# The output product of a soft mixture of experts: 16 small float32 tiles in place of two passes of a rounded pair

## The chip, the core and the metric

The kernel runs on one core of a Trainium2 chip. A core has a matrix engine (TensorE, PE in the profile; its weight loads are shown apart as PEld), a vector engine (VectorE, DVE), a scalar engine (ScalarE, ACT), GpSimd (POOL) and a queue that issues transfers (SyncE, SP). Each engine works through its own instructions in order and waits on semaphores for the others. TensorE writes to PSUM, 128 partitions of eight banks of 512 float32 values; everything else lives in SBUF, the on-chip memory. The metric is the device time in microseconds of one execution; a profiled execution also gives a span, from the first to the last instruction.

## The reference

The input `x` has shape (8, 2496, 256). The real part of its two-dimensional Fourier transform is the token matrix of a soft mixture of experts with eight experts of four slots:

```python
X = np.fft.fft(np.fft.fft(x, axis=1), axis=2).real   # reshaped to N = 19968 rows of 256
logits = X @ phi                                      # N x 32
d = softmax of logits over the rows;  slot_input = d.T @ X        # 32 x 256
for e in range(8):                                    # four slots each
    slot_out[e] = relu(slot_input[e] @ w1[e]) @ w2[e]
c = softmax of logits over the 32 slots
return c @ slot_out                                   # N x 256
```

Both softmaxes add 1e-9 to the denominator. Only the last line is computed differently by the change: a product of N x 32 weights with a 32 x 256 matrix, which writes 20.45 MB.

## The kernel before

The eight sequences are handled as four pairs `p` = 0 to 3. The kernel never forms the transformed tokens. It works on folded input, gets the logits of a pair (`lt[p]`) through small transforms, collects the slot inputs, runs the experts, and then weights the expert outputs for every token.

The code is cut into parts, `a`, `t`, `b`, `c`, `e`, `d`, `u` for the transforms and sums of a pair, `m`, `l`, `v` for the experts, and four that matter here. The string `ORDER` lists them in the order in which they are written, and a scheduler with a time model then sets the order on each engine.

- `part_r` takes the finished slot outputs `so` from PSUM (L508, L509), repeats them with one product (`sorep`, L510), and builds the right-hand matrices `rh`. They are in float32r, a format that TensorE takes in one pass; since it is rounded, `rh[0]` holds the value and `rh[1]` what the rounding lost (L515), each with two copies of the 32 x 256 matrix on a block diagonal.
- `part_s(p)` is the softmax over the slots: eleven TensorE transposes of the logits into three PSUM banks (`cT`, L529), three ScalarE copies into `c` (L534), and then for each of two halves a maximum (VectorE, L543), a subtract (POOL, L544), an exponential (ScalarE, L545), a sum, an addition and a reciprocal (VectorE, L546 to L548), and a product (POOL, L549).
- `part_q(p, i)` splits half `i` of `c` into a float32r value (ScalarE, L555) and its residual (VectorE, L556), side by side in `hl`.
- `part_o(p, b)` is one chunk of output, five for each pair. Four TensorE transposes turn a block of `hl` into weights (`lT`, L569), ScalarE copies them to SBUF (`lTs`, L570), and four times two products with `rh` (L576) fill one bank each, `po`, 128 x 512. VectorE and ScalarE copy the banks in turn to a buffer `o` (L580), and SP sends it (L587, L585), 1 MiB for a whole chunk.

The buffers `o` come from a ring of six; they are reused when their transfer has landed. PSUM is split into pools that live through the whole kernel: `ps` (two banks), `ps3` (three), `p1` (two) and `u` (one). The products `po` use `ps` and `ps3`, the transposes `cT` and `lT` use `p1`.

In `ORDER` the end reads `... q00 s10 v00 v10 r00 o00 q01 o01 q10 o02 o03 o04 o10 s20 q11 o11 ...`: the softmaxes of pairs 0 and 1 come ahead of the experts' end, those of pairs 2 and 3 between the chunks.

Of the kernel before, what the change touches and what calls it, by code (L numbers as in the profile page):

```python
# [116 lines left out]
def _build(nc, tc, xh, phih, w1h, w2h, cins, where, out, out0):  # L117
# [4 lines left out]
    with ctx:  # L122
        cp = ctx.enter_context(tc.tile_pool(name="cp", bufs=1))
        sb = ctx.enter_context(tc.tile_pool(name="sb", bufs=1))
        pp = ctx.enter_context(tc.tile_pool(name="pp", bufs=P2, space=PSUM))
# [373 lines left out]

        def part_r():  # L500
            so = sos_[0]
            for j in range(2):
# [5 lines left out]
            sc.copy(sos[:, :128], so[:, :128])  # L508
            v.tensor_copy(sos[:, 128:], so[:, 128:D])  # L509
# [2 lines left out]
            sc.copy(rh[0][half[0], 0, :], ps[half[0], :D])
# [8 lines left out]

        def part_s(p):
            L = lt[p]
            cq[p] = sb.tile([128, 40, NSLOT], F32, name=f"c{p}", tag=CT[p], bufs=bufs_(CT[p]))
# [13 lines left out]
            e1 = nc.gpsimd if GP & 1 else v  # L538
            e2 = nc.gpsimd if GP & 2 else v
            for i in range(2):  # L540
# [3 lines left out]
                e1.tensor_tensor(c, c, m[:, 0].unsqueeze(2).to_broadcast([128, 20, NSLOT]), op=ALU.subtract)  # L544
# [4 lines left out]
                e2.tensor_tensor(c, c, m[:, 1].unsqueeze(2).to_broadcast([128, 20, NSLOT]), op=ALU.mult)  # L549

        def part_q(p, i):
            c = cq[p][:, 20 * i : 20 * i + 20]
            e3 = nc.gpsimd if GP & 4 else v
# [2 lines left out]
            e3.tensor_tensor(t[:, :, 1], c, t[:, :, 0].bitcast(F32), op=ALU.subtract)  # L556
# [4 lines left out]

        def part_o(p, b):
            ps = bank1(f"lT{p}_{b}", F32R)
            lT = et([128, 4, 128], f"lTs{p}_{b}", F32R)
            with tc.issue_after(anchor["v1"]) if LA and p == 0 else nullcontext():
              for i in range(4):
                k0 = 8 * b + 2 * i
                src = hl[p, k0 // 20][:, k0 % 20 : k0 % 20 + 2].rearrange("p k h s -> p (k h s)")
                pe.transpose(ps[:, i * 128 : i * 128 + 128], src, identr)  # L569
            sc.copy(lT, ps.rearrange("p (i n) -> p i n", i=4))  # L570
# [87 lines left out]
```

## Time and profile before

| | us |
|---|---|
| three runs of the kernel | 199.41, 200.8, 201.35 |
| the profiled execution | 201.22 |
| its span | 199.4 |
| PE busy (share of the span) | 174.7 (88%) |
| DVE busy | 131.8 (66%) |
| ACT busy | 132.4 (66%) |
| POOL busy | 24.6 (12%) |
| experts' last product ends, about | 139.5 |
| first output transfer is issued | 143.90 |
| last output transfer is issued | 190.89 |

The profile's rows give an engine, a line of the kernel, the operation, output and input tiles and a count, and then times: in the groups, busy us and mean ns of one, and the engine's idle time ahead of them with what ended it; in the timeline and the chain, start and length in us. A busy TensorE is not TensorE at its peak, since matmuls overlap and their ends are modelled.

### The profile page before, as it was taken

What the parts mean: (1) busy time and instruction counts of PE and PEld (TensorE: products, weight loads), DVE (VectorE), ACT (ScalarE), POOL (GpSimd) and SP (SyncE); (2) the same over time, 40 slices, a digit from 0 to 9 for tenths busy, and PEclk for the clock granted to TensorE, in tenths of its full rate; (3) what the DMA queues carried; (4) which work ended last, traced back from release to release, by engine and by line L of the source; (5) the groups of instructions that cost most, each with busy time, mean ns of one, the idle gap of its engine ahead of it and who ended that gap; (6) DMA issues with size and microseconds to landing.
All of it is one profiled execution on the core that took longest, in us unless ns stands there. A gap on an engine that the chain in (4) does not pass through costs nothing.

```text
span 199.4 us, 4290 instructions
## 1 busy us (share of the span) xinstructions
PE 174.7 (88%) x1690; PEld 125.6 (63%) x1690; DVE 131.8 (66%) x238; ACT 132.4 (66%) x277; POOL 24.6 (12%) x27
## 2 busy tenths in 40 slices
PE   0499889969999999989999989999999999989900
PEld 0375575549666877556865859346788877768700
DVE  0599856989993991742357624796677888976700
ACT  2135775579876795687856963763867988896610
POOL 0000000000000000000000100767101357320000
PEclk9999999997999999999999999999999999999995
DMA  5999999998880499600393687991099999799996
GB/s 183 409 427 410 422 420 420 419 391 291 301 363 21 112 358 424 263 0 0 111 283 138 205 326 234 364 404 58 2 378 355 419 409 389 306 421 363 430 426 214
DMA packets 10707, 59.17 MB, mean 297 GB/s; under 512 B 1344, under 2 KB 1728, under 8 KB 5696
## 3 DMA queue, kind: packets, MB, share of 16 engines
q1 hardware_dynamic: 10688, 58.91, 76.0%
q8 instruction: 13, 0.21, 0.4%
q14 instruction: 6, 0.05, 0.1%
HBM read 38.46 MB, written 20.45 MB: 295 GB/s over the span
## 4 chain that ended last, share of the span: by engine, by line
PE 75%; ACT 10%; DMA 2%; DVE 2%; issue 2%; POOL 2%; SPq 0%; ACTq 0%; DVEq 0%; POOLq 0%
PE po L576 17%; PE pt L231 9%; PE z L238 7%; PE a L275 6%; PE e L331 6%; PE u L373 5%; PE d L348 4%; PE h L472 4%; PE so L492 3%; PE lp L293 3%; PE lm L294 3%; PE cT L529 2%; DMA x<-xh 2%; ACT zt L262 2%; PE lT L569 2%
## 5 line engine op out<-in xcount | busy, mean ns | idle before, releaser
L576 PE MATMUL po<-rh,lTs 128*128 128x512 f32 x160 | 42.4, 405 | 1.5 <-ACT lTs L570 0.7
L231 PE MATMUL pt<-cs,eo 128*128 128x128 f32 x160 | 26.9, 300 | 8.9 <-DVE eo L226 7.9
L576 PEld LDWEIGHTS po<-rh,lTs 128*128 128x128 f32 x160 | 28.1, 188 | 8.5 <-ACT o L580 1.8
L232 ACT COPY et<-pt 128x512 f32<-128x512 f32 x40 | 23.1, 592 | 13.8 <-PE pt L231 13.2
L580 DVE COPY o<-po 128x512 f32<-128x512 f32 (+1 forms) x40 | 26.9, 686 | 7.9 <-PE po L576 7.0
L231 PEld LDWEIGHTS pt<-cs,eo 128*128 128x128 f32 x160 | 19.9, 153 | 15.9 <-DVE eo L226 7.9
L580 ACT COPY o<-po 128x512 f32<-128x512 f32 x40 | 23.2, 595 | 7.3 <-PE po L576 7.1
L224 DVE TENSOR_TENSOR x<-x 128x1024 f32<-128x1024 f32 x16 | 19.5, 1217 | 3.0 <-DMA x<-xh 3.0
L238 PE MATMUL z<-et,wphi 128*32 128x256 f32 (+1 forms) x288 | 19.0, 371 | 1.9 <-ACT et L232 1.8
L544 POOL TENSOR_TENSOR c<-c,cm 128x640 f32<-128x640 f32 x8 | 11.8, 1489 | 28.0 <-DVE cm L543 27.0
L316 ACT ACTIVATE d<-lt,nm 120x128 f32<-120x128 f32 x44 | 13.6, 390 | 1.9 <-DVE nm L313 1.8
L226 DVE TENSOR_TENSOR eo<-x 128x512 f32<-128x512 f32 x20 | 13.6, 682 | 0.6 <-PE u L373 0.3
L238 PEld LDWEIGHTS z<-et,wphi 128*32 128x32 f32 x288 | 7.8, 113 | 9.4 <-ACT et L232 4.2
L227 DVE TENSOR_TENSOR eo<-x 128x512 f32<-128x512 f32 x20 | 13.6, 680 | 0.0
L331 PE MATMUL e<-cs,dpm 120*64 120x120 f32 x176 | 13.5, 273 | 0.0
L331 PEld LDWEIGHTS e<-cs,dpm 120*64 120x64 f32 x176 | 10.7, 136 | 3.5 <-issue 2.4
L356 ACT COPY ds<-d 64x320 f32<-64x320 f32 x24 | 10.0, 421 | 4.2 <-PE d L348 3.5
L275 PE MATMUL a<-cs,zt 128*120 128x128 f32 x88 | 12.2, 292 | 0.4 <-ACT zt L266 0.3
L275 PEld LDWEIGHTS a<-cs,zt 128*120 128x120 f32 x88 | 11.1, 196 | 1.9 <-ACT zt L266 1.3
L549 POOL TENSOR_TENSOR c<-c,cm 128x640 f32<-128x640 f32 x8 | 11.0, 1391 | 10.0 <-DVE cm L548 5.5
L570 ACT CAST lTs<-lT 128x512 fp32r<-128x512 f32 x20 | 11.5, 599 | 0.9 <-PE lT L569 0.9
L373 PE MATMUL u<-eo,ds 128*32 128x129 f32 x320 | 11.6, 275 | 0.0
(99 smaller groups left out, 251.4 us busy)
## 6 DMA issues: line engine op xcount, KB each, us to landing
x<-xh SPq DMA_DIRECT2D x16, 1024.0 KB, 11.3
out<-o SPq DMA_DIRECT2D x15, 1024.0 KB, 5.6
w<-w1h SPq DMA_DIRECT2D x6, 1024.0 KB, 8.6
w<-w2h SPq DMA_DIRECT2D x12, 512.0 KB, 6.0
x<-xh SPq DMA_DIRECT2D x4, 896.0 KB, 10.3
out<-o SPq DMA_DIRECT2D x4, 768.0 KB, 6.0
w<-w1h SPq DMA_DIRECT2D x4, 512.0 KB, 5.2
w<-w2h SPq DMA_DIRECT2D x2, 1024.0 KB, 8.0
```

The lines of the kernel that those rows point to most:

```text
L224: v.tensor_tensor(x[:, 0:4], x[:, 0:4], x[:, 4:8], op=ALU.add)
L226: v.tensor_tensor(e[:, :, 0:128], x[:, 0:4, 0:128], x[:, 0:4, 128:256], op=ALU.add)
L227: v.tensor_tensor(e[:, :, 128:256], x[:, 0:4, 0:128], x[:, 0:4, 128:256], op=ALU.subtract)
L231: pe.transpose(b[:, g * 128 : g * 128 + 128], e[:, g, k * 128 : k * 128 + 128], ident)
L232: sc.copy(tr[k][:, :, :, qi, :], b.rearrange("p (g h a) -> p g h a", g=4, h=2))
L238: pe.matmul(z[32 * g : 32 * g + 32, o : o + n], wphi[:, w, :], tr[k][:, g].rearrange("p h q a -> p (h q a)"), start=i != 1, stop=i != 0, t ...
L275: pe.matmul(ps[:120, i * 128 : i * 128 + 128], zt[p][:, GS * g : GS * g + GS].rearrange("p s h c -> p (s h c)"), C("wa"), start=True, stop ...
L316: sc.activation(d[:, g], L[:, g], AF.Exp, bias=nm[:, g : g + 1], scale=1.0)
L331: pe.matmul(ps[64 * k : 64 * k + 64, 120 * i : 120 * i + 120], dpm[p, hf][:, k, 3 * j + i, :], C(name), start=True, stop=True, tile_positi ...
L373: last = pe.matmul(ub[32 * g : 32 * g + 32, 0:129], dsb[p][:, k, c, :], e[:, 0:129] if k == 0 else e[:, 127:256], start=cc == 0, stop=cc == 9,
L576: pe.matmul(po, lT[:, i, :], rh[j].rearrange("p k d -> p (k d)"), start=j == 0, stop=j == 1,)
L580: (v.tensor_copy if n_ev[0] % 2 else sc.copy)(ot[:np_, 2 * i : 2 * i + 2, :].rearrange("p k d -> p (k d)"), po[:np_])
```

## The change

The output product is done in plain float32, with 32 x 32 tiles of the array. `part_q` is one VectorE transpose of a half of `c`, which turns 32 x 32 blocks and leaves them where they are, so that the slots of quarter `q` of the partitions come to lie on partitions 32q to 32q + 31 (`tl`). `part_o` then has 32 products for each chunk: row tile `q` takes 32 weights' rows on the partitions of quarter `q` and the copy of the slot outputs that lies there (`rep`), column tile `j` writes 32 partitions, and row tile `q` writes bank `q`. A chunk fills a slot of four banks; ScalarE copies banks 0 and 1, VectorE banks 2 and 3, 1024 values wide each. The two slots take all eight banks, so the pools from before are closed in `part_r`, and the logits' transposes of pairs 2 and 3 (`cT2`, `cT3`) use such a slot too. The splitting into value and residual, the identity in float32r, the `lT` transposes and their copies go. The order of rows in the output buffer differs, and the host puts them in place.

```diff
+        def four(name):
+            return p4[0].tile([128, 4, 512], F32, name=name, tag="p4")
...
         def part_r():
...
-            sc.copy(rh[0][half[0], 0, :], ps[half[0], :D])
-            (v.tensor_copy if RH else sc.copy)(rh[0][half[1], 1, :], ps[half[1], :D])
-            for k, r in enumerate(half):
-                v.tensor_tensor(rh[1][r, k, :], ps[r, :D], rh[0][r, k, :].bitcast(F32), op=ALU.subtract)
+            sc.copy(rep[:, :128], ps[:, :128])
+            v.tensor_copy(rep[:, 128:], ps[:, 128:D])
+            rep_.append(rep)
+            banks.close()
+            p4.append(ctx.enter_context(tc.tile_pool(name="p4", bufs=2, space=PSUM)))
...
         def part_s(p):
+            whole = four(f"cT{p}") if p4 else None
             for b in range(3):
-                ps = bank1(f"cT{p}_{b}")
+                ps = whole[:, b] if p4 else bank1(f"cT{p}_{b}")
...
         def part_q(p, i):
-            sc.copy(t[:, :, 0], c)
-            e3.tensor_tensor(t[:, :, 1], c, t[:, :, 0].bitcast(F32), op=ALU.subtract)
+            if i == 0:
+                tl[p] = se([128, 2 * NKC, NSLOT], f"tl{p}")
+            half = slice(20 * i, 20 * i + 20)
+            v.transpose(
+                tl[p][:, half].rearrange("p k n -> p (k n)"), cq[p][:, half].rearrange("p k n -> p (k n)")
+            )
...
         def part_o(p, b):
-            for i in range(4):
-                po = (bank, bank3)[i % 2](f"po{p}_{b}_{i}")
-                for j in range(2):
-                    pe.matmul(
-                        po, lT[:, i, :], rh[j].rearrange("p k d -> p (k d)"), start=j == 0, stop=j == 1,
+            po = four(f"po{p}_{b}")
+            for gi in range(2):
+                for j in range(4):
+                    for q in range(4):
+                        r = slice(32 * q, 32 * q + 32)
+                        pe.matmul(
+                            po[32 * j : 32 * j + 32, q, 256 * gi : 256 * gi + 256],
+                            tl[p][r, 8 * b + 4 * gi + j, :], rep[r, :],
+                            start=True, stop=True, tile_position=(32 * q, 32 * j),
+                        )
...
+            for i, ev in ((0, sc.copy), (1, v.tensor_copy)):
+                src = po[:, 2 * i : 2 * i + 2]
+                if b < 4 or i == 0:
+                    ev(ot[:, 4 * i : 4 * i + 4].rearrange("p k d -> p (k d)"), src.rearrange("p q n -> p (q n)"))
```

Three places in the engines' orders, with what each instruction waits for (a semaphore bears the name of the engine that raises it; DMAHW are transfers). First VectorE where the experts end and the output begins, before; `c1` are the weights of pair 1, `so` the slot outputs:

```order
L546 TENSOR_REDUCE cm1_1_1598<-c1_1572 128x20 [waits Activation_49]
L547 TENSOR_SCALAR cm1_1_1598<-cm1_1_1598 128x20 [waits DVE_49]
L548 RECIPROCAL cm1_1_1598<-cm1_1_1598 128x20 [waits DVE_49]
L556 TENSOR_TENSOR hl1_0_1740<-c1_1572,hl1_0_1740 128x20x32 [waits Activation_49]
L509 COPY sos_1676<-so_1606 128x128 [waits Activation_49]
L515 TENSOR_TENSOR rh1_1673<-sorep_1677,rh0_1671 64x256 [waits PE_49,Activation_49]
```

And there after the change:

```order
L543 TENSOR_REDUCE cm1_1_1596<-c1_1570 128x20 [waits Activation_49]
L553 STREAM_TRANSPOSE tl1_1759<-c1_1570 128x640 [waits Pool_49]
L544 TENSOR_SCALAR cm1_1_1596<-cm1_1_1596 128x20 [waits DVE_49]
L545 RECIPROCAL cm1_1_1596<-cm1_1_1596 128x20 [waits DVE_49]
L553 STREAM_TRANSPOSE tl1_1759<-c1_1570 128x640 [waits Pool_49]
L509 COPY sos_1669<-so_1604 128x128 [waits Activation_49]
L512 COPY rep_1670<-sorep_1671 128x128 [waits Activation_49]
```

Both transposes of pair 1, which wait for POOL, now stand ahead of the copy of `so`; before, the second half's subtract stood behind it. Second, the softmax of pair 2, on VectorE before; `po1_1_1` is a bank of the second chunk of pair 1:

```order
L543 TENSOR_REDUCE cm2_0_1862<-c2_1844 128x20 [waits Activation_49]
L543 TENSOR_REDUCE cm2_1_1870<-c2_1844 128x20 [waits DVE_49]
L580 COPY o1_0_1826<-po1_0_1_1831 128x512 [waits DMAHW3_49,DMAHW0_49,PE_49]
L580 COPY o1_0_1826<-po1_0_3_1839 128x512 [waits PE_49]
L580 COPY o1_1_1888<-po1_1_1_1893 128x512 [waits DMAHW3_49,DMAHW2_49,DMAHW4_49,DVE_49,PE_49]
L580 COPY o1_1_1888<-po1_1_3_1901 128x512 [waits PE_49]
L546 TENSOR_REDUCE cm2_0_1862<-c2_1844 128x20 [waits Activation_49]
L580 COPY o1_2_1916<-po1_2_1_1921 128x512 [waits DMAHW5_49,DVE_49,PE_49]
```

And there after, up to the copy of the third chunk of pair 1:

```order
L540 TENSOR_REDUCE cm2_0_1926<-c2_1910 128x20 [waits Activation_49]
L540 TENSOR_REDUCE cm2_1_1934<-c2_1910 128x20
L543 TENSOR_REDUCE cm2_0_1926<-c2_1910 128x20 [waits Activation_49]
L544 TENSOR_SCALAR cm2_0_1926<-cm2_0_1926 128x20 [waits DVE_49]
L545 RECIPROCAL cm2_0_1926<-cm2_0_1926 128x20 [waits DVE_49]
L543 TENSOR_REDUCE cm2_1_1934<-c2_1910 128x20 [waits Activation_49]
L575 COPY o1_1_1976<-po1_1_1943 128x1024 [waits DMAHW3_49,DMAHW2_49,Activation_49]
L544 TENSOR_SCALAR cm2_1_1934<-cm2_1_1934 128x20 [waits DVE_49]
L553 STREAM_TRANSPOSE tl2_1980<-c2_1910 128x640 [waits Pool_49]
L545 RECIPROCAL cm2_1_1934<-cm2_1_1934 128x20 [waits DVE_49]
L553 STREAM_TRANSPOSE tl2_1980<-c2_1910 128x640 [waits Pool_49]
L575 COPY o1_2_2015<-po1_2_1982 128x1024 [waits DMAHW4_49,Activation_49]
```

Before, copies of chunks stand between the steps of the softmax, and each waits for PE. After, all steps up to the second sum stand ahead of the next chunk's copy, and that copy waits for ScalarE's copy of the same chunk. ScalarE at the same place, before:

```order
L580 COPY o1_0_1826<-po1_0_0_1827 128x512 [waits DMAHW3_49,DMAHW0_49,PE_49]
L545 ACTIVATE c2_1844<-c2_1844 128x640 [waits Pool_49]
L580 COPY o1_0_1826<-po1_0_2_1835 128x512 [waits PE_49]
L570 COPY lTs1_3_1935<-lT1_3_1934 128x512 [waits PE_49]
L545 ACTIVATE c2_1844<-c2_1844 128x640 [waits Pool_49]
L580 COPY o1_1_1888<-po1_1_0_1889 128x512 [waits DMAHW3_49,DMAHW2_49,DMAHW4_49,DVE_49,PE_49]
```

And after:

```order
L575 COPY o1_0_1906<-po1_0_1873 128x1024 [waits DMAHW3_49,DMAHW0_49,PE_49]
L533 COPY c2_1910<-cT2_1911 128x40x12 [waits PE_49] x2
L533 COPY c2_1910<-cT2_1911 128x40x8 [waits PE_49]
L542 ACTIVATE c2_1910<-c2_1910 128x640 [waits Pool_49] x2
L575 COPY o1_1_1976<-po1_1_1943 128x1024 [waits DMAHW2_49,DMAHW3_49,DVE_49,PE_49]
```

Here too a chunk's copy now stands behind both exponentials. Third, TensorE at the logits' transposes of pair 2, before:

```order
L576 MATMUL po0_3_2_1784<-rh0_1671,lTs0_3_1769 128x512 [waits Activation_49]
L576 MATMUL po0_3_2_1784<-rh1_1673,lTs0_3_1769 128x512
L529 MATMUL cT2_1_1851<-cs0_70,lt2_943 128x120 [waits PE_49,Activation_49]
L529 MATMUL cT2_1_1851<-cs0_70,lt2_943 128x120 x3
L529 MATMUL cT2_2_1857<-cs0_70,lt2_943 128x120 [waits Activation_49]
L529 MATMUL cT2_2_1857<-cs0_70,lt2_943 128x120 x2
```

And after:

```order
L528 MATMUL cT2_1911<-cs0_70,lt2_942 128x120 [waits DVE_49]
L528 MATMUL cT2_1911<-cs0_70,lt2_942 128x120 x3
L528 MATMUL cT2_1911<-cs0_70,lt2_942 128x120 [waits Activation_49]
L528 MATMUL cT2_1911<-cs0_70,lt2_942 128x120 x3
L566 MATMUL po1_1_1943<-rep_1670,tl1_1759 32x256 [waits DVE_49]
L566 MATMUL po1_1_1943<-rep_1670,tl1_1759 32x256 x15
L528 MATMUL cT2_1911<-cs0_70,lt2_942 128x120 [waits Activation_49]
```

Before, the groups took the two banks of `p1` in turn, so that one could be filled while the other was read. Now the three lie in one slot, whose first group waits for VectorE to free it, and each later group waits for ScalarE's copy of the group ahead.

More of the change, by code (lines that the diff above doesn't have):

```diff
@@ L498, in part_v @@
             anchor[f"v{eh}"] = ins.ins
+        rep_ = []
         def part_r():
             so = sos_[0]
-            for j in range(2):
-                rh.append(sb.tile([128, 2, D], F32R, name=f"rh{j}", tag="d", bufs=2))
-                nc.gpsimd.memset(rh[j].bitcast(F32), 0.0)
-            v.tensor_copy(identr, ident)
             sos = sb.tile([128, D], F32, name="sos", tag="dpm", bufs=2)
+            rep = sb.tile([128, D], F32, name="rep", tag="d", bufs=2)
             ps = bank("sorep")
@@ L510, in part_r @@
             pe.matmul(ps[:, :D], C("sel2"), sos, start=True, stop=True)
-            half = [slice(0, 64), slice(64, 128)]
-            sc.copy(rh[0][half[0], 0, :], ps[half[0], :D])
-            (v.tensor_copy if RH else sc.copy)(rh[0][half[1], 1, :], ps[half[1], :D])
-            for k, r in enumerate(half):
-                v.tensor_tensor(rh[1][r, k, :], ps[r, :D], rh[0][r, k, :].bitcast(F32), op=ALU.subtract)
-        identr = sb.tile([128, 128], F32R, name="identr", tag="mex2", bufs=1)
-        hl, cq = {}, {}
+            sc.copy(rep[:, :128], ps[:, :128])
[3 more added lines that the diff above has]
+            p4.append(ctx.enter_context(tc.tile_pool(name="p4", bufs=2, space=PSUM)))
+        tl, cq = {}, {}
         def part_s(p):
@@ L556, in part_q @@
-            e3.tensor_tensor(t[:, :, 1], c, t[:, :, 0].bitcast(F32), op=ALU.subtract)
-            hl[p, i] = t
-        n_ev = [0]
-        def part_o(p, b):
-            ps = bank1(f"lT{p}_{b}", F32R)
-            lT = et([128, 4, 128], f"lTs{p}_{b}", F32R)
-            with tc.issue_after(anchor["v1"]) if LA and p == 0 else nullcontext():
-              for i in range(4):
[L567 to L570, printed above, removed]
-            ot = ring(f"o{p}_{b}")
-            done = 0
-            for i in range(4):
-                po = (bank, bank3)[i % 2](f"po{p}_{b}_{i}")
-                for j in range(2):
-                    pe.matmul(
-                        po, lT[:, i, :], rh[j].rearrange("p k d -> p (k d)"), start=j == 0, stop=j == 1,
-                    )
-                np_ = 64 if b == 4 and i == 3 else 128
-                (v.tensor_copy if n_ev[0] % 2 else sc.copy)(
-                    ot[:np_, 2 * i : 2 * i + 2, :].rearrange("p k d -> p (k d)"), po[:np_]
-                )
-                n_ev[0] += 1
-                if b == 4 and i == 3:
-                    nc.sync.dma_start(out0[p].rearrange("p (r d) -> p r d", d=D), ot[:64, 6:8])
-                elif i == 3 or (b == 4 and i == 2) or ((p, b) == (0, 0) and i in FIRST):
@@ L644 @@
     r = _run(nc, [arrays], core_ids=[0])
-    got = r.results[0]["out"].reshape(NPAIR, 2, NA, 19, 2, D)
-    got0 = r.results[0]["out0"].reshape(NPAIR, NA, 2, D)
+    rows = r.results[0]["out"].reshape(NPAIR, 4, 32, 38, D).transpose(0, 3, 2, 1, 4)
+    rest = r.results[0]["out0"].reshape(NPAIR, 2, 32, 2, D).transpose(0, 3, 2, 1, 4)
+    place = np.zeros((NPAIR, 4, 32, 10, 4, D), np.float32)
+    for q in range(4):
+        for g in range(9):
+            row = 8 * (g // 2) + 2 * q + g % 2 if g < 8 else (32, 34, 36, 37)[q]
+            place[:, q, :, g] = rows[:, row]
+        if q < 2:
+            place[:, q, :, 9] = rows[:, 33 + 2 * q]
+        else:
+            place[:, q, :, 9, :2] = rest[:, q - 2]
+    place = place.reshape(NPAIR, 2, NA, NKC, 2, D)
+    got, got0 = place[:, :, :, :19], place[:, 0, :, 19]
     full = np.empty((NPAIR, 2, 2496, D), np.float32)
```

37 lines of the change are left out of this document (18 added, 19 removed).

## The prediction

> **What bounds the kernel now.** I read the page's head and its 40 slices, then the stretches of the last 55 us, then the chain and the timeline around the start of the output stage, then the groups by form for prices. The last part of the span is the output stage: it ships 20.45 MB (the page's "written 20.45 MB").
>
> ```profile
> span 199.4 us, 4290 instructions
> ...
> DMA  5999999998880499600393687991099999799996
> GB/s 183 409 427 410 422 420 420 419 391 291 301 363 21 112 358 424 263 0 0 111 283 138 205 326 234 364 404 58 2 378 355 419 409 389 306 421 363 430 426 214
> ...
> HBM read 38.46 MB, written 20.45 MB: 295 GB/s over the span
> ```
>
> The reader should see that after slice 28 (2 GB/s) the transfers are nearly always busy. The stretches say it more finely; columns are the stretch, its length, busy time (instructions) of PE, PEld, DVE, ACT and POOL, granted clock, DMA share, GB/s.
>
> ```profile
> core 0: us, PE busy (x) PEld busy (x) DVE busy (x) ACT busy (x) POOL busy (x), PEclk, DMA share, GB/s
> 144.00:154.00 10.00, 10.00 (x56) 8.25 (x55) 7.23 (x12) 7.38 (x14) 0.11 (x1) 1.00 0.87 340
> 154.00:164.00 10.00, 10.00 (x60) 8.18 (x58) 8.37 (x17) 8.99 (x18) 4.88 (x4) 1.00 1.01 418
> 164.00:174.00 10.00, 9.51 (x51) 7.01 (x51) 9.22 (x18) 8.87 (x17) 4.64 (x3) 1.00 0.86 347
> 174.00:184.00 10.00, 9.30 (x52) 7.42 (x51) 6.79 (x10) 8.16 (x16) 1.53 (x2) 1.00 1.00 391
> 184.00:194.00 10.00, 5.76 (x27) 4.06 (x25) 4.05 (x6) 4.26 (x8) 0.00 (x0) 1.00 1.02 426
> 194.00:199.40 5.40, 0.00 (x0) 0.00 (x0) 0.00 (x0) 0.00 (x0) 0.00 (x0) 0.53 0.66 237
> ```
>
> PE is busy here too, but the transfers are full: in three of the stretches their share is 1.00 or more, at 418, 391 and 426 GB/s, mean 412. At that rate the output needs 20.45/0.412 = 49.6 us, 2.55 us for a chunk of 1 MiB, whatever PE does. The last byte leaves at about 194 + 0.66 x 5.4 = 197.6. So before has at most some 3 us of free transfer time to win, and the change is judged by two questions: when do the transfers start, and do they run dry?
>
> **The start.**
>
> ```profile
> 138.77 1.68 POOL L549 TENSOR_TENSOR c<-c,cm 128x640 f32<-128x640 f32 x1 [1.07 <-DVE cm L548]
> ...
> 139.85 0.29 DVE L509 COPY sos<-so 128x128 f32<-128x128 f32 x1 [0.53 <-ACT sos L508]
> ...
> 140.96 0.37 ACT L512 CAST rh<-sorep 64x256 fp32r<-64x256 f32 x1
> ...
> 143.29 1.27 ACT L580 COPY o<-po 128x512 f32<-128x512 f32 x2 [0.21 <-PE po L576]
> ...
> 143.90 0.35 SPq L587 DMA_DIRECT2D out<-o  x1
> ```
>
> These are the steps to the first output transfer at 143.90. The copy of `sos` on VectorE starts 0.03 us after ScalarE's half: two readers of one PSUM tile go one behind the other.
>
> **Prices.** From the groups by form (count | busy us, mean ns | idle before, releaser), one row of the timeline, two of the chain (start, us) and one of the transfers' issues (count, size, us to landing):
>
> ```profile
> L580 DVE COPY o<-po 128x512 f32<-128x512 f32 x36 | 24.2, 687 | 6.8 <-PE po L576 6.0
> L224 DVE TENSOR_TENSOR x<-x 128x1024 f32<-128x1024 f32 x16 | 19.5, 1217 | 3.0 <-DMA x<-xh 3.0
> L246 ACT COPY zs<-z 128x512 f32<-128x512 f32 x8 | 4.7, 583 | 6.2 <-PE z L238 6.2
> L246 ACT COPY zs<-z 128x256 f32<-128x256 f32 x4 | 1.7, 414 | 0.8 <-PE z L238 0.8
> L484 DVE STREAM_TRANSPOSE hT<-hs 128x512 f32<-128x512 f32 x4 | 2.7, 678 | 0.1
> L556 DVE TENSOR_TENSOR hl<-c,hl 128x640 fp32r<-128x640 f32 x8 | 7.1, 883 | 0.0
> L543 DVE TENSOR_REDUCE cm<-c 128x20 f32<-128x640 f32 x8 | 6.2, 809 | 1.7 <-ACT c L534 1.7
> L545 ACT ACTIVATE c<-c 128x640 f32<-128x640 f32 x8 | 6.0, 749 | 3.3 <-POOL c L544 3.2
> L534 ACT COPY c<-cT 128x480 f32<-128x480 f32 x8 | 4.4, 565 | 3.8 <-PE cT L529 3.8
> L534 ACT COPY c<-cT 128x320 f32<-128x320 f32 x4 | 1.7, 433 | 0.2 <-PE cT L529 0.2
> L548 DVE RECIPROCAL cm<-cm 128x20 f32<-128x20 f32 x8 | 2.2, 270 | 0.1
> L547 DVE TENSOR_SCALAR cm<-cm 128x20 f32<-128x20 f32 x8 | 1.3, 158 | 0.1
> L492 PE MATMUL so<-w,hT 128*32 128x256 f32 x128 | 7.7, 379 | 0.0
> L570 ACT CAST lTs<-lT 128x512 fp32r<-128x512 f32 x20 | 11.5, 599 | 0.9 <-PE lT L569 0.9
> ...
> 153.89 2.50 POOL L544 TENSOR_TENSOR c<-c,cm 128x640 f32<-128x640 f32 x2 [13.45 <-DVE cm L543]
> ...
> 133.65 5.84 PE so L492 x109
> ...
> 148.83 0.41 PE cT L529 x4
> ...
> out<-o SPq DMA_DIRECT2D x2, 256.0 KB, 2.2
> ```
>
> *A chunk's matmuls.* L492 has 64 calls in the code and x128 rows: a float32 product is two passes. The chain has 109 passes in 5.84 us, 53.6 ns each, on four column tiles of 256 columns: 0.214 us for one pass, a quarter of it when four tiles share the array. A new chunk is 32 calls, 64 passes of the same width. No row of before uses row tiles, so two bounds: all 16 tiles at once, 64 x 0.214/16 = 0.86 us; never more than four at once, 64 x 53.6 ns = 3.43 us. I take 0.86, because the trace charges four tiles exactly a quarter each, with no floor showing; with 0.38 for the last matmul's own duration a fill is 1.24. [...]
>
> *Evictions.* 1024 wide: VectorE 1.20 (687 for 512, and L224, with one input more, takes 1217 for 1024), ScalarE 0.93 (583 plus twice the 169 between the two L246 rows). In the order after, VectorE's copy of a chunk waits for ScalarE's of the same chunk, so they add. A slot is taken for 1.24 + 0.93 + 1.20 + three hand-overs of 0.05 = 3.5 us, and two slots give a chunk every 1.76 us, under the 2.55 of the transfer. The removed `lT` transposes, `lTs` casts (599 ns) and residual subtracts (883) count nothing, since the transfers beside them were full (if they ran dry there, the cast would give 0.6 a chunk back). The dropped memset and cast of the identity lay in idle time of POOL and VectorE.
>
> *Later start.* After, both transposes of pair 1 stand ahead of the `sos` copy on VectorE. The second waits for POOL's product, 138.77 + 1.68 = 140.45 (that product may come 0.4 sooner, half of 2.50, without a subtract beside it, or 0.8 later, since a transpose now precedes pair 1's maximum); transpose 0.82 (678 ns for 512, scaled to 640), copy 0.29: 141.6. From the end of `sos` to the first read of `sorep` is 0.82 (140.14 to 140.96): 142.4; two `rep` copies, one behind the other, 0.6: 143.05; fill 1.24, ScalarE 0.93: first issue at 145.3, **+1.4 us**. VectorE's half is out at 146.5.
>
> *First dry spell.* Six chunks come before pair 2's softmax, the sixth at 146.5 + 5 x 1.76 = 155.3. I put 1.0 us from an issue to flowing data (of the 2.2 us in which 256 KB landed 0.64 are moving at 412 GB/s; I take 1.0 of the rest as ahead), so data flows from 146.3, and 6.16 MB are gone at 161.3. Meanwhile `cT2` takes the slot that chunk 5 leaves at 153.6. Its three rounds no longer overlap (TensorE waits for ScalarE's copy of the round before): 0.41 for four transposes and the 0.21 that L580 waited behind PE make 0.62; three times that with 0.565, 0.565 and 0.433 is 3.5, with hand-overs 157.2. Then maximum 0.81, two POOL subtracts 2.5, exponential 0.75: 161.4. Only then, in both queues' order, are ScalarE (0.93) and VectorE (1.20) free for `o1_1`: 163.6, data at 164.7. **Dry 3.4.**
>
> *Second.* Behind it VectorE has scalar, transpose, reciprocal (0.16 + 0.82 + 0.27), POOL's product (1.25) that needs that reciprocal, and a transpose, all ahead of `o1_2`: 163.6 + 1.3 + 1.3 + 0.85 + 1.2 = 168.3, data 169.3, against 164.7 + 2.55 = 167.2. **Dry 2.1.**
>
> *Pair 3.* `cT3` gets its slot at 169.5, but ScalarE must first copy `o1_4` (170.5); the same chain gives `o2_0` at 179.7, data 180.8, while three chunks from 169.3 last until 176.6. **Dry 4.2**, and 2.1 again behind it.
>
> *Sum.* 146.3 + 49.6 + 3.4 + 2.1 + 4.2 + 2.1 = 207.7 for the last byte against 197.6: +10.1. Before spent 197.6 - 144.9 = 52.7 on the same bytes, so its own 3.1 of dry time is taken off in this. What follows the last byte is unchanged. The profiled execution took 201.22, so 211.3 us; it is 0.2% above the runs' median 200.8.
>
> **Rivals.**
>
> *Not slower: the backlog covers the softmax.* Chunks outrun the transfers, so the queue may never run dry. Then only the start and before's own gaps count: 201.2 + 1.4 - 3.1 = 199.5. It decides where the chain from `cT2` to `o1_1`'s transfer is at most the 7.7 us left in the queue at 153.6; I get 11.1. Against it: every link is a row above. For it: the two engines' order might allow it if my hand-overs are too dear. 199 to 203 us.
>
> *A fill of about 1.7 to 2.2 us.* Either row tiles overlap only in part, or the clock falls while TensorE waits. The row of 194.00:199.40, without a matmul, has a clock of 0.53. With fills and transposes twice as long: start +0.9, period 2.2, sixth chunk 3.0 later, `cT` 1.2 longer, so the dry spells grow by about 3.3 and 1.6: 217 us. [...] In my sum most fills have slack under the 2.55 of a transfer, so a slow restart lies inside the range.
>
> *Row tiles do not overlap.* 3.43 a chunk is above 2.55: TensorE becomes the bound. 143.05 + 20 x 3.43 + some 4 at each softmax + 6 behind the last fill (its copies, issue and transfer) = 226, +28: about 230 us.
>
> **Numbers.** Forecast as summed 0.63, its own range 207 to 215. Fill 1.7 to 2.2: 0.17. No row overlap: 0.11. Backlog covers: 0.09, mostly within 1%. The range 207 to 219 leaves out the last two. Slower by over 1% 0.91, within 1% 0.06, faster 0.03; about 1% is what a measurement of this kernel can tell from no change.
>
> **What would show it.** DMA slices with two pairs of dips, near 161 to 169 and 176 to 185, and full ones between; first output issue near 145.3; VectorE's 128x1024 copies released by ScalarE; `o1_1`'s copy released by POOL or the exponential; 64 passes of a chunk in about 0.9 us. If passes are 53 ns apart, the row-tile term is wrong; if slices stay full through 160 to 185, the backlog rival holds.

## The result and the profile after

The changed kernel takes 215.81 us (median of 4 runs, 215.46 to 216.26) against 200.92 us before (4 runs, 199.41 to 201.35): a ratio of 1.078, with a 95% interval of 1.073 to 1.083. The forecast was 211.3 us, in a range of 207 to 219. The profiled execution took 216.26 us, 0.45 above its median.

First the head of the page and two rows of its slices (a slice is 5.36 us here).

```profile
span 214.4 us, 6261 instructions
...
PEclk9999999999999999999999999997998558559885
DMA  6999999989913993008629599105994692479995
```

The transfers, nearly always busy from slice 29 on before, now have two pairs of holes, in slices 30 to 31 and 33 to 35. In the same slices the granted clock of TensorE stands at five to eight tenths; before, it stood at 1.00 in this stage until 194 and fell only behind the last matmul (0.53 in 194 to 199.4). The stretches put lengths on the holes (length, busy time of each engine, clock, DMA share, GB/s):

```profile
148.00:151.00 3.00, 2.41 (x115) 1.28 (x95) 2.12 (x2) 1.31 (x2) 0.00 (x0) 1.00 0.78 310
162.00:167.00 5.00, 1.55 (x51) 1.04 (x64) 4.18 (x8) 2.57 (x4) 2.20 (x3) 0.77 0.44 181
168.00:171.00 3.00, 1.17 (x38) 0.71 (x42) 2.91 (x3) 0.88 (x1) 0.00 (x0) 0.50 0.40 158
177.00:186.00 9.00, 4.80 (x160) 2.32 (x129) 5.73 (x10) 3.55 (x5) 4.95 (x4) 0.69 0.30 110
186.00:190.00 4.00, 2.00 (x71) 1.21 (x66) 3.08 (x3) 1.01 (x1) 0.06 (x1) 0.50 0.58 240
...
204.00:214.40 10.40, 1.30 (x35) 0.36 (x7) 2.45 (x2) 1.66 (x2) 0.00 (x0) 0.66 0.75 305
```

What a share lacks to 1.00 is dry time: 3.0 x 0.22 = 0.7 us at the start, then 2.8, 1.8, 6.3 and 1.7 us, 13.3 in all. Before lost 3.1 on the same bytes by the prediction's account, slow places included. The last row puts the last byte at 204 + 0.75 x 10.4 = 211.8, against 197.6. Now the steps to the first transfer, from the timeline (start, duration, idle before and what ended it):

```profile
139.48 1.26 POOL L546 TENSOR_TENSOR c<-c,cm 128x640 f32<-128x640 f32 x1 [1.39 <-ACT sos L508]
140.77 0.84 DVE L553 STREAM_TRANSPOSE tl<-c 128x640 f32<-128x640 f32 x1 [1.44 <-POOL c L546]
141.54 0.25 DVE L509 COPY sos<-so 128x128 f32<-128x128 f32 x1
...
143.23 4.02 PE L566 MATMUL po<-rep,tl 32*32 32x256 f32 x128 [0.68 <-DVE rep L512]
145.18 1.01 ACT L575 COPY o<-po 128x1024 f32<-128x1024 f32 x1 [2.33 <-PE po L566]
146.22 1.60 SPq L583 DMA_DIRECT2D out<-o  x2
```

The copy of `sos` waits for the transpose and the transpose for POOL, at 141.54 where 141.6 was forecast. The first issue comes at 146.22 (143.90 before). The groups of the copies:

```profile
L575 ACT COPY o<-po 128x1024 f32<-128x1024 f32 x20 | 19.9, 1011 | 28.3 <-PE po L566 28.3
L575 DVE COPY o<-po 128x1024 f32<-128x1024 f32 x16 | 19.2, 1216 | 14.8 <-ACT o L575 14.7
```

VectorE's idle time ahead of its copies is ended by ScalarE's copy in 14.7 of 14.8 us: the two halves of a slot go one behind the other.

### The profile page after: what moved, and what is told of

Same layout as the page of the kernel before. It is cut to its first block, busy times and chain, and to the rows that moved or that the text cites. A ratio compares the mean times of both kernels' runs of the same rounds, so it can differ in the third digit from the quotient of the medians.

```text
span 214.4 us, 6261 instructions
## 1 busy us (share of the span) xinstructions
PE 166.8 (78%) x2730; PEld 109.2 (51%) x2730; DVE 129.3 (60%) x216; ACT 114.8 (54%) x228; POOL 20.8 (10%) x25
## 4 chain that ended last, share of the span: by engine, by line
PE 62%; ACT 14%; DVE 10%; issue 4%; POOL 2%; DMA 2%; POOLq 1%; SPq 0%; ACTq 0%; DVEq 0%
PE po L566 9%; PE pt L232 9%; PE z L239 6%; PE e L332 5%; PE a L276 5%; PE u L374 5%; ACT o L575 4%; DVE o L575 4%; PE d L349 4%; PE h L472 3%; PE so L492 3%; PE cT L528 3%; PE lp L294 3%; PE lm L295 2%; DMA x<-xh 2%
## 5 line engine op out<-in xcount | busy, mean ns | idle before, releaser
L566 PE MATMUL po<-rep,tl 32*32 32x256 f32 x1280 | 37.0, 489 | 19.5 <-DVE o L575 16.4
L566 PEld LDWEIGHTS po<-rep,tl 32*32 32x32 f32 x1280 | 19.9, 117 | 34.4 <-DVE o L575 22.7
L575 ACT COPY o<-po 128x1024 f32<-128x1024 f32 x20 | 19.9, 1011 | 28.3 <-PE po L566 28.3
L233 ACT COPY et<-pt 128x512 f32<-128x512 f32 x40 | 23.2, 595 | 14.2 <-PE pt L232 13.7
L575 DVE COPY o<-po 128x1024 f32<-128x1024 f32 x16 | 19.2, 1216 | 14.8 <-ACT o L575 14.7
L541 POOL TENSOR_TENSOR c<-c,cm 128x640 f32<-128x640 f32 x8 | 10.0, 1263 | 81.2 <-DVE cm L540 81.2
L276 PE MATMUL a<-cs,zt 128*120 128x128 f32 x88 | 11.3, 279 | 1.0 <-ACT zt L267 0.9
L276 PEld LDWEIGHTS a<-cs,zt 128*120 128x120 f32 x88 | 10.2, 183 | 2.4 <-ACT zt L267 1.8
L298 DVE TENSOR_TENSOR lt<-lt,lm 120x384 f32<-120x384 f32 (+1 forms) x8 | 4.1, 517 | 12.0 <-PE lm L295 12.0
L546 POOL TENSOR_TENSOR c<-c,cm 128x640 f32<-128x640 f32 x8 | 10.1, 1262 | 9.0 <-DVE cm L545 7.6
```

Of the source, the lines that this page charges most:

```text
L233: sc.copy(tr[k][:, :, :, qi, :], b.rearrange("p (g h a) -> p g h a", g=4, h=2))
L276: pe.matmul(ps[:120, i * 128 : i * 128 + 128], zt[p][:, GS * g : GS * g + GS].rearrange("p s h c -> p (s h c)"), C("wa"), start=True, stop ...
L566: pe.matmul(po[32 * j : 32 * j + 32, q, 256 * gi : 256 * gi + 256], tl[p][r, 8 * b + 4 * gi + j, :], rep[r, :], start=True, stop=True, til ...
L575: ev(ot[:, 4 * i : 4 * i + 4].rearrange("p k d -> p (k d)"), src.rearrange("p q n -> p (q n)"))
```

## The experiments

The theories at the start. A: the transfers run dry because the softmaxes of pairs 2 and 3 stand between the chunks' copies, with the slots making copies and `cT` rounds serial. B: the product itself is too slow. C: the halved clock lengthens what TensorE does in the spells. D came up on the way: TensorE stands still for its code. Each kernel was compared with the kernel before on its own chip, so the ratios are what is to be compared with 1.078; the medians of that kernel differ from chip to chip by up to 0.9 us (200.03 to 200.93), and differences in us below carry that. "The changed kernel" is the one this case is about.

| run | us | ratio to before, 95% interval |
|---|---|---|
| changed kernel | 215.81 | 1.073 to 1.083 |
| e1 softmaxes ahead of the stage | 212.48 | 1.055 to 1.067 |
| e2 slots of two banks | 213.95 | 1.059 to 1.071 |
| e3 slots of one bank | 213.36 | 1.058 to 1.069 |
| e8 products repeated | 221.34 | 1.098 to 1.109 |
| e10 one transpose later | 214.33 | 1.061 to 1.071 |
| e9 own banks for cT | 209.47 | 1.039 to 1.047 |
| e8b fewer repeats | 215.44 | 1.066 to 1.076 |
| e4 every product twice | 248.71 | 1.231 to 1.242 |
| e11 softmaxes moved, two banks | 207.01 | 1.031 to 1.039 |
| e12 softmaxes moved, four banks | 207.78 | 1.035 to 1.045 |
| e13 wide products | 213.79 | 1.066 to 1.075 |
| e14 softmax of pair 3 earlier | 206.52 | 1.020 to 1.035 |

### e1: both softmaxes ahead of the output stage

```
-    ... v00 v10 r00 o00 ... o04 o10 s20 q11 o11 ... o14 s30 o20 ...
+    ... v00 s20 v10 s30 r00 o00 ... o04 o10 q11 o11 ... o14 o20 ...
```

> The softmaxes of pairs 2 and 3 are written ahead of the output stage; the product, its slots and the copies stay as in the changed kernel. Theory A (the transfers run dry because the softmaxes of pairs 2 and 3 stand between the chunks' copies): no dry spell of more than 1 us is left behind the first issue, so the 12.3 us of the four spells go, and the first issue comes later by what the moved work does not find idle, about 8 us (near 154): last byte near 154 + 1 + 49.6 = 205, time near 209 against 215.8. Theory B (the product or its copies are too slow to feed the transfers, softmax or not): spells stay between the chunks and the later start is paid on top, 220 or more. Theory C (the halved TensorE clock): the clock should still fall wherever TensorE has nothing but one fill of 1.5 us in 2.55, and fills of 2.4 should leave the time at 209 all the same, since a fill is still shorter than a transfer.

212.48 us. From the page and the timeline:

```profile
PEclk9999999999999999999999999997559996587975
DMA  5999999999904993008719699300078999899994
...
152.41 3.01 SPq L583 DMA_DIRECT2D out<-o  x3
```

The first issue is 6.2 us later than in the changed kernel, and behind it no slice falls below seven tenths until the end. The clock is halved in places here too (slice 34, say), and the transfers keep 0.8 there, as C expected for a stage in which a fill has 2.55 us. So A holds: without softmaxes between the copies, the same product, slots and copies feed the transfers. B does not: spells do not stay. It came out 3.5 above the 209 of A, for the transfers still slow down in places (in 157 to 161 their share is 0.81); no run here settles why.

### e2 and e3: the slots

e2 makes two slots of two banks from each slot of four, so that ScalarE's and VectorE's copies belong to different tiles. e3 gives each row tile a bank of its own and copies 512 elements at a time, alternating:

```
-            po = four(f"po{p}_{b}")
+            po = [four(f"po{p}_{b}_{i}") for i in range(2)]    # e3: range(4), one bank each
...
-                            po[32 * j : 32 * j + 32, q, 256 * gi : 256 * gi + 256],
+                            po[q // 2][32 * j : 32 * j + 32, q % 2, 256 * gi : 256 * gi + 256],
```

> Each slot of four banks becomes two of two banks, one for ScalarE's copy and one for VectorE's; the product is the same. Theory A with the serial copies as its second half: VectorE's copy no longer waits for ScalarE's, each of the four spells is shorter by about 1 us and the cT rounds run one ahead, so 12.3 us of spells become 8 to 9 and the time is near 211. Rival (the softmax chain alone sets the spells, the slots nothing): 214.5 to 216. Theory B (the product): unchanged, 216.

> The product on 16 tiles stays, each row tile has a bank of its own, and the copies are 512 wide and alternate between ScalarE and VectorE as they did before the change. That undoes the slots of four banks alone. If the slots are what costs: near 202 to 205. If it is the softmaxes' place in the engines' order (which is still between the chunks' copies): two spells of 3 to 5 us stay and the time is near 209. If it is the product: 214 to 217.

213.95 and 213.36 us. Undoing the slots gives back 1.9 and 2.4 us; e2 fell between its 211 and the 214.5 to 216 of its rival. In e3 two long spells are left (first row, 6.0 x 0.72 = 4.3 us, and 8.0 x 0.72 = 5.8):

```profile
162.00:168.00 6.00, 3.61 (x98) 2.00 (x73) 5.19 (x9) 1.28 (x3) 2.35 (x2) 0.78 0.28 113
176.00:184.00 8.00, 2.25 (x37) 1.03 (x38) 6.77 (x12) 2.51 (x5) 3.30 (x3) 0.77 0.28 106
```

My expectation for e3 gave 209 if the softmaxes' place is what costs and 214 if it is the product; it fell nearer the second. The cause is in the order: with single banks the scheduler put VectorE's two copies of `o1_1` behind the whole softmax of pair 2. The serial copies are a small part of the loss, and e3 alone could not say which of the two others is the large one.

### e9: banks of their own for cT

The logits keep the two single banks of `p1`, and the chunks get three slots of two banks:

```
+        p1 = ctx.enter_context(tc.tile_pool(name="p1", bufs=P1, space=PSUM))
         banks = ctx.enter_context(ExitStack())
...
-            p4.append(ctx.enter_context(tc.tile_pool(name="p4", bufs=2, space=PSUM)))
+            p4.append(ctx.enter_context(tc.tile_pool(name="p4", bufs=3, space=PSUM)))
...
-                ps = whole[:, b] if p4 else bank1(f"cT{p}_{b}")
+                ps = bank1(f"cT{p}_{b}")
```

> As the run with slots of two banks, but with three of those slots, and the transposed logits cT of every pair keep two single banks of their own, as before the change. Theory A, sharper (cT2 and cT3 come late because they must take a slot in turn behind the chunks; with banks of their own they are ready before the output stage): both softmaxes move ahead of the second chunk, one stretch of some 5 us between 150 and 158 is partly dry, none behind it: near 207 to 208, against 213.95 with two-bank slots that cT shares. Rival (the spells are the softmaxes' work as such, wherever it stands): 212 to 215.

209.47 us, 4.5 below e2, which has the same slots but lets `cT` take its turn in them. The stretches:

```profile
144.00:156.00 12.00, 6.75 (x175) 3.76 (x160) 9.76 (x17) 5.02 (x6) 7.77 (x7) 0.70 0.32 130
156.00:196.00 40.00, 31.26 (x1046) 18.86 (x1040) 22.17 (x21) 16.07 (x17) 0.00 (x0) 0.92 0.99 395
```

Both softmaxes ran ahead of the second chunk, the price is one dry stretch there, and then the transfers are full for 40 us. The time is 1.5 to 2.5 us above the 207 to 208 that I expected. This names what the change took away from the softmaxes: before, `cT` had two banks that no chunk used; now a slot comes round to it only behind five chunks' copies.

### e10: the start

The second transpose of pair 1 (`x11`) is issued behind VectorE's copy of `rep`:

```
-    ... v10 r00 o00 q01 o01 q10 o02 o03 o04 o10 s20 q11 o11 ...
+    ... v10 r00 o00 q01 o01 q10 x11 o02 o03 o04 o10 s20 o11 ...
...
-            v.tensor_copy(rep[:, 128:], ps[:, 128:D])
+            anchor["r"] = v.tensor_copy(rep[:, 128:], ps[:, 128:D]).ins
...
+        def held(f, *a):
+            with tc.issue_after(anchor["r"]):
+                return f(*a)
```

> The changed kernel with the second transpose of pair 1 held behind the copy of rep on VectorE; every other instruction stays in its place. If the start's term is right (the copy of sos waits for that transpose, which waits for POOL's product), sos is copied 1.2 to 1.4 us sooner, the first issue comes that much sooner and, since nothing in the spells depends on it, so does everything behind: near 214.5 against 215.8. Rival (the first spell only grows by what the start wins, because the softmax of pair 2 does not move with it): 215.5 to 216.

214.33 us, 1.5 less, as expected:

```profile
139.87 0.29 DVE L509 COPY sos<-so 128x128 f32<-128x128 f32 x1 [0.16 <-ACT sos L508]
...
144.17 2.85 SPq L583 DMA_DIRECT2D out<-o  x3
```

VectorE's copy of `sos` started at 139.87 instead of 141.54, the first issue came at 144.17 instead of 146.22, and the spells stayed. The first issue won 0.4 us more than `sos` did: the first 128 passes took 2.75 us here instead of 4.02, and ScalarE's copy came 1.54 us behind their start instead of 1.95.

### e8, e8b and e13: the clock

e8 issues the products of four chunks again, into the same places; e8b does so for two chunks, once; e13 puts wide products, thrown away, ahead of the four chunks:

```
-            for gi in range(2):
+            for gi in [0, 1] * {(1, 2): 4, (1, 3): 2, (2, 1): 4, (2, 2): 2}.get((p, b), 1):    # e8b: {(1, 2): 2, (2, 1): 2}
```

```
             po = four(f"po{p}_{b}")
+            for q in range({(1, 2): 4, (1, 3): 2, (2, 1): 4, (2, 2): 2}.get((p, b), 0)):
+                pe.matmul(po[:, q % 4, :], ident, tl[p].rearrange("p k n -> p (k n)")[:, :512], start=True, stop=True)
```

> The changed kernel with the products of four chunks issued again into the same places (o1_2 and o2_1 four times, o1_3 and o2_2 twice), in the stretches in which TensorE idles; nothing else moves in any engine's order. Theory C (the clock halves because TensorE idles, and the halved clock lengthens the third spell): the granted clock stays at 1.00 from 160 to 192, the fill of o1_4 takes 1.5 instead of 2.4 and the cT3 rounds 0.63 instead of 1.06, so o2_0's transfer comes some 2.2 us sooner: near 213.5. Rival (the clock does not matter to the time, the chain of softmaxes and copies does): 215 to 216. If the clock falls for another reason than idling, it still falls, and the time is 216 or more.

> The run that repeated the products four times came out at 221.3 although the clock stayed at 1.00, because the repeats outran their gap: 128 passes took 4.0 to 4.3 us there, 1.3 to 1.7 of it waits of TensorE that the trace calls issue, beside transfers of 16 KB on the queue for instructions. Here the products of o1_2 and o2_1 are issued only twice, which should end near 163, ahead of ScalarE's copy at 164. Theory C (the halved clock lengthens the third spell): the clock falls later than at 164.7 or not at all in that stretch, and the time is 1 to 2.2 us below the changed kernel's, 213.6 to 214.8. Rival: the clock does not matter, 215.3 to 216.3.

> The changed kernel with a few wide products (128 x 128 by 128 x 512, thrown away) ahead of the chunks that stand before TensorE's long waits: four ahead of o1_2 and o2_1, two ahead of o1_3 and o2_2. They keep TensorE busy with 24 instructions where the repeats needed hundreds, and should end before the copies come; every other engine's order stays. Theory C: the clock stays at 1.00 through 161 to 178, o1_4's fill takes 1.5 instead of 2.4 and the stretch from cT3's first round to the end of o2_0's copies about 10.0 instead of 11.5 (it took 10.0 in the run with four repeats, at full clock): some 2.4 us sooner, near 213.4. Rival (the clock is not what lengthens the third spell): 215 to 216.5.

e8 took 221.34 us. Its clock stayed at 1.00 from 160 to 194, but the repeats outran their gap, because of waits that the trace calls issue:

```profile
164.18 2.75 PE L566 MATMUL po<-rep,tl 32*32 32x256 f32 x128 [1.73 <-issue]
168.18 2.77 PE L566 MATMUL po<-rep,tl 32*32 32x256 f32 x128 [1.26 <-issue]
```

e8b took 215.44, with an interval (1.066 to 1.076) that overlaps the changed kernel's (1.073 to 1.083), and the clock stood at 0.53 in 164 to 174, as in the changed kernel, with TensorE busy for 5.92 of those 10 us (5.89 there), so it tells nothing on C. e13 did what e8 was meant to. Two of its stretches, three rows of its timeline, and the rows of the changed kernel that answer to these:

```profile
164.00:174.00 10.00, 7.01 (x201) 3.52 (x200) 7.01 (x12) 4.79 (x6) 2.53 (x2) 1.00 0.54 220
...
177.00:186.00 9.00, 7.77 (x137) 3.43 (x138) 5.93 (x11) 3.39 (x4) 5.01 (x4) 1.00 0.51 199
```

```profile
171.04 1.49 PE L570 MATMUL po<-rep,tl 32*32 32x256 f32 x64 [0.98 <-DVE o L579]
172.46 0.63 PE L528 MATMUL cT<-cs,lt 120*128 120x120 f32 x4
...
182.97 0.34 SPq L587 DMA_DIRECT2D out<-o  x1
```

```profile
169.84 2.38 PE L566 MATMUL po<-rep,tl 32*32 32x256 f32 x64 [2.00 <-DVE o L575]
172.14 1.06 PE L528 MATMUL cT<-cs,lt 120*128 120x120 f32 x4
...
183.69 11.42 SPq L583 DMA_DIRECT2D out<-o  x5
```

At full clock the fill of `o1_4` takes 1.49 instead of 2.38 and a `cT` round 0.63 instead of 1.06; from that fill to `o2_0`'s issue it is 11.93 us instead of 13.85, and the third spell is 9.0 x 0.49 = 4.4 us instead of 6.3. So the halved clock makes the third spell about 1.9 us longer. The median fell by 2.0 us, or by 1.1 when each is taken above the kernel before on its own chip, and the two intervals overlap (1.066 to 1.075 and 1.073 to 1.083); the profiled execution, 215.52, is only 0.7 below the changed kernel's 216.26, for the fill of `o1_4` began 1.2 us later there. So what the clock costs in time is not shown; the stretch is the better evidence. The other spells did not shrink: 163 to 168 was 2.85 us dry.

### e4: every product twice

```
-                    for q in range(4):
+                    for q in [q for q in range(4) for _ in range(2)]:
```

> Every product of the output stage is issued twice, and nothing else changes. What does one fill really cost? If its 64 passes cost only what they take at full clock, 1.1 to 1.5 us, a chunk of 128 passes takes 2.6, about a transfer's 2.55, and only the spells and the start grow: 220 to 224. If TensorE cannot get its code faster than 256 instructions (128 passes with their weight loads) in 4.0 to 4.3 us, as the four-times run showed it, TensorE becomes the bound: 20 chunks of 4.1 us from 143.2 are 82 us, and with the waits at the two softmaxes and some 6 us behind the last fill the time is 231 to 238.

248.71 us, above both cases. Eight chunks in a row:

```profile
205.68 33.91 PE L566 MATMUL po<-rep,tl 32*32 32x256 f32 x1024 [2.53 <-DVE o L575]
```

33.1 ns a pass at a clock of 0.97 (mean of 208 to 244), 4.24 us for a chunk, which is what the expectation's second case took (4.0 to 4.3), but the trace shows no stop of the kind seen in e8. The doubled calls follow each other on the same tile, which the single ones do not; e8's repeats, a whole sweep over the 16 tiles apart, ran 128 passes in 2.75 us, 21.5 ns each between two stops. So this run may measure the order of the calls as much as their number, and does not answer what one fill costs. That code comes too slowly here is not excluded: with its stops e8 takes 4.0 to 4.3 us for 128 passes. It is no evidence on the changed kernel.

### e11 and e12: the softmaxes moved inside the stage

e12 has three edits of place: the softmax of pair 2 ahead of the copies of `sos`, that of pair 3 behind `o1_1` in the code, and e10's. e11 has the slots of two banks besides.

```
-    ... v10 r00 o00 q01 o01 q10 o02 o03 o04 o10 s20 q11 o11 q20 o12 o13 q21 o14 s30 o20 ...
+    ... v10 s20 r00 o00 q01 q10 o01 x11 o02 o03 o04 o10 o11 s30 q20 o12 o13 q21 o14 o20 ...
```

(`x11` is the second transpose of pair 1, held as in e10.)

> Three edits together on the same product: the softmax of pair 2 is written ahead of the copies of sos, that of pair 3 behind o1_1, the second transpose of pair 1 is held behind rep's copy, and the slots are of two banks. Theory A: the first issue comes near 146, no spell of more than 1 us is left, so the last byte leaves at about 147 + 49.6 + 0.5 + the 2 to 3 us by which the transfers slow down here and there in all these runs, 199 to 200: time 202.5 to 205. If the product itself (its fills, its code, the halved clock) costs more than the places of the softmaxes and the slots: 208 or more.

> The same without the smaller slots: softmax of pair 2 ahead of the copies of sos, that of pair 3 behind o1_1, the second transpose of pair 1 behind rep's copy, slots of four banks. Theory A with the slots as its second half: one spell is left, at the softmax of pair 3 near 170, of about 5 us, so 5 us above the run with two-bank slots, 207.5 to 210. Rival (the slots matter little once the softmaxes are moved): within 1.5 us of it.

207.01 and 207.78 us. Moving the softmaxes gives 6.5 us on top of e10 (214.33 to 207.78, ratios 1.066 and 1.040), with the slots of four banks left as they are; taken above the kernel before on its own chip it is 5.7. The slots then make 0.8 us between the medians, and the intervals overlap: the rival of e12 was right, not A's second half. And 207 misses the 202.5 to 205 that A promised, as it misses the 208 or more of the other case. A spell is left in both, at 164 to 170: 6.0 x 0.70 = 4.2 us in e11, 6.0 x 0.65 = 3.9 in e12. TensorE's rows ahead of it in e11:

```profile
151.85 3.19 PE L566 MATMUL po<-rep,tl 32*32 32x256 f32 x128 [0.41 <-issue]
158.60 1.15 PE L566 MATMUL po<-rep,tl 32*32 32x256 f32 x26 [3.55 <-issue]
159.68 1.66 PE L528 MATMUL cT<-cs,lt 120*128 120x120 f32 x7
...
163.14 1.06 PE L528 MATMUL cT<-cs,lt 120*128 120x120 f32 x4
```

After 128 passes TensorE stands still for 3.55 us with nothing to wait for that the profile shows, and `cT3` comes 26 passes behind that. In the stretch 156.2 to 157.6, the transfers show one on the queue for instructions:

```profile
q1 hardware_dynamic: 88, 0.56, 97.1%
q8 instruction: 1, 0.02, 4.2%
```

By its share, 4.2% of 16 engines' 1.4 us, that transfer takes 0.94 us, and it is over by the end of the stretch; TensorE goes on at 158.60, 1.0 us behind that. The table of waits gives "issue" 12.1 us of TensorE in five pieces in e11.

e12 has no such stop there. Its rows at the same place, and its spell:

```profile
155.94 1.86 PE L566 MATMUL po<-rep,tl 32*32 32x256 f32 x64 [1.09 <-DVE o L577]
...
157.73 0.63 PE L528 MATMUL cT<-cs,lt 120*128 120x120 f32 x4
```

```profile
164.00:170.00 6.00, 1.69 (x66) 1.06 (x68) 4.64 (x8) 3.29 (x4) 3.79 (x4) 0.91 0.35 142
```

`cT3` begins 2 us sooner than in e11, TensorE waits only for a slot ahead of it, and the spell is as long.

### e14: cT3 ahead of the stop

```
-    ... o02 o03 o04 o10 o11 s30 q20 o12 ...
+    ... o02 o03 o04 s30 o10 o11 q20 o12 ...
```

> The moved kernel with two-bank slots (207.0) with one edit: the softmax of pair 3 is written behind o04 instead of behind o11. There TensorE stood still 3.55 us, which the trace calls issue, after 128 passes in a row, until a 16 KB transfer on the queue for instructions had landed; cT3 came 26 passes behind that stop, and the one spell left (165 to 169) follows it. Here cT3 stands about 128 passes sooner, ahead of that stop. Theory D (the stops for code make cT3 late): cT3's rounds run near 153 to 156 instead of 159.7 to 164, the spell shrinks to 1 us or less, time 203.5 to 205. Rival (the spell is the softmax's own work between the copies, wherever the stop falls): it only moves ahead, where fewer chunks are in the queue, 207 to 209.

206.52 us (four runs: 205.17, 205.76, 207.27, 207.47). The rounds of `cT3` now run at 154.20 and 156.34, as D had it, and the spell is 3.0 x 0.34 = 1.0 us:

```profile
154.20 0.94 PE L528 MATMUL cT<-cs,lt 120*128 120x120 f32 x7
...
156.34 0.63 PE L528 MATMUL cT<-cs,lt 120*128 120x120 f32 x4
...
176.52 4.09 PE L566 MATMUL po<-rep,tl 32*32 32x256 f32 x128 [4.02 <-issue]
```

```profile
160.00:163.00 3.00, 1.82 (x67) 0.82 (x64) 2.00 (x5) 2.99 (x5) 0.98 (x1) 1.00 0.66 244
```

But the time fell by 0.5 us, within the intervals. The profiled run's first issue was 1.3 us later than e11's (146.77 against 145.49), and further stops, the longest 4.02 us, stand in the last 30 us, where the transfers fall to a share of 0.91 and 0.82 in two stretches of 10 us that had 1.01 and 0.92 in e11. The time lies between D's 203.5 to 205 and its rival's 207 to 209. The spell went, as D had it, but the edit moved `cT3` ahead of some 128 passes as well as of the stop, and in e12 a spell of 3.9 us stands without the stop. So the softmax's place can account for the spell by itself; that the stop made it is not shown. No version here beats the kernel before.

## Why the prediction was right, and where its sizes were off

The sign, the mechanism and the places were right; the time came out 4.5 us above the forecast, inside the range of 207 to 219 but 0.8 above the likeliest case's own range.

| term of the sum | forecast | measured |
|---|---|---|
| copy of `sos` on VectorE | 141.6 | 141.54 |
| first issue | 145.3 | 146.22 |
| fill of a chunk | 1.24 | 1.49 at full clock, 2.38 at half |
| copy of 1024, ScalarE, VectorE | 0.93, 1.20 | 1.01, 1.22 |
| first and second spell | 3.4, 2.1 | 2.8, 1.8 |
| third and fourth spell | 4.2, 2.1 | 6.3, 1.7 |
| last byte | 207.7 | 211.8 |

*The later start.* Shown by e10: the transpose ahead of `sos` is worth 1.5 us of time. The forecast of the first issue was 0.9 too early: 0.7 of that is the first fill, 1.95 us where 1.24 stood, with the clock at half from 144.17 on, 0.1 ScalarE's copy, and the rest a fill that began at 143.23 instead of 143.05.

*The fill.* All 16 tiles do run at once: the first 16 passes of a chunk start within 0.12 us. At half clock 64 passes start over 1.75 us (2.38 less the last one's 0.63), 27.3 ns each, a sixteenth of twice 0.214 us as the prediction's lower bound has it. At full clock they start over 1.12 us (1.49 less 0.37), 17.5 ns each in the mean and not the 13.4 of that bound. The mean hides a stop: the first 33 start over 0.46 us, 14 ns apart, then none for 0.19 us, and the rest come about 16 ns apart; at half clock there is a stop of 0.24 us at the same pass. No run here shows what makes it. The prediction's reason for its bound, that four tiles are charged exactly a quarter each, was circular, since its 0.214 was itself 4 x 53.6; it is the trace after that bears it out, where the second 16 passes of a chunk start 0.427 us behind the first 16 at half clock, twice 0.214.

*The serial copies.* They are there (14.7 us of VectorE's idle time), but they were overrated as a cause. Undone in e2 they give 1.9 us, and 0.8, within the intervals, once the softmaxes are elsewhere.

*The spells.* The main term, 11.8 us forecast and 12.6 measured in these four, with 0.7 more at the start that I did not see. e1, e9 and e11 show that they come from the softmaxes' place. The third is the one that was mis-sized, by 2.1 us. The step that failed was that `cT3` gets its slot at 169.5 and then waits only for ScalarE's copy of `o1_4`, until 170.5: in TensorE's order the fill of `o1_4` also stands ahead of `cT3`, it began at 169.84 and took 2.38 us at half clock, and ScalarE's first copy of `cT3` came at 173.24. e13 puts 1.9 us of it on the clock.

*What follows the sum.* 147.2 for the first data, 49.6 of transfers and 13.3 of spells make 210.1; the last byte left at 211.8. The 1.7 between are mostly transfers that slow down without stopping (398 and 395 GB/s in 151 to 162 and 190 to 204, against the 412 of the forecast), which the sum had no term for. Against before, the start is 2.3 us later and 15.0 us are lost behind it instead of 3.1, which make the 14.2 between the two last bytes.

*The rivals.* The fill of 1.7 to 2.2 us, with a falling clock as one of its two causes, came half true. The granted clock is halved in four stretches of the stage (0.53 of full in 164 to 174), and the fills of `o1_3`, `o1_4` and `o2_2` took 2.38; its 217 us is 1.2 too many, since at full clock a fill is 1.49. The other two are excluded: passes are 17.5 ns apart and not 53, and the queue ran dry. The four halved stretches begin at 144.17, 164.65, 181.72 and 202.20 and last 3.4, 13.7, 10.2 and 3.4 us; e13, with TensorE busy for 7.0 to 8.5 us of every 10 between 154 and 194 (5.5 to 7.5 in the changed kernel), has none there. How long a pause makes the clock fall, and how much work holds it, is not shown.

*What stays open.* e11 and e14 are still 7.0 and 5.6 us above the kernel before. In e11, 1.6 of it is the first issue (145.49 against 143.90). The rest is one spell and slow places in the transfers, beside the stops that the trace calls issue (12.1 us in all); I could not take the stops away without changing the product, so their price, also in the changed kernel, where the profile shows only 1.9 us of them, is not measured.

## What to carry to other kernels

When one pool of large PSUM slots replaces several small ones, look at who now has to take a turn in it. Here the softmax of the next pair lost its own two banks, came behind five chunks' copies, and that cost more than the serial copies (4.5 us from e2 to e9, against 1.9); what the product itself costs stays open. Cost a slot's round by who stands in it, in the order in which the tiles are taken, and put work with a long chain behind it (here 11.5 us from `cT3`'s first round to the next transfer) ahead of the stage that must not run dry, or give it banks of its own.

## What the runs showed of the hardware

*Stops of TensorE beside transfers of instructions.* The changed stage issues 1280 passes with as many weight loads. Transfers on the queue for instructions, from the pages of before and of after:

```profile
q8 instruction: 13, 0.21, 0.4%
```

```profile
q8 instruction: 21, 0.34, 0.6%
```

Each is 16,384 bytes. In e11, e14 and e8 TensorE stops for 0.4 to 4.0 us where nothing that the profile shows holds it. From stop to stop the timelines count 128, 512, 128 and 128 matmuls in e11, 256 and four times 128 in e14, and 128 or 256 in e8. The changed kernel has two such stops, of 0.91 and 1.04 us, 128 matmuls apart; they end at 196.43 and 201.80, 1.50 and 1.21 us behind the end of such a transfer (194.93 and 200.59). Another 16.4 us of TensorE's waits in its stage end with VectorE's copy of a slot; whether a stop lies under some of those is not shown. In e11, with the output's transfers at 97% of the same engines in 156.2 to 157.6, the stop was 3.55 us. That TensorE waits for its code in these stops is my reading of where they lie; no run here shows it by itself.

*Two calls on one tile in a row may be dear.* e4 took 33.1 ns a pass against 21.5 in e8's repeats between two stops, both on 16 tiles. That the order of the calls makes it is argued from these two runs and not shown; a slow supply of code is the rival.
